# Gated linear attention and two mixtures: lo parts of the first weights on VectorE, gates cumulated in one float32 product, new ranks for the first phase

## The chip, the cores and the metric

The kernel runs on one core of a Trainium2 chip. The metric is the device time of one execution in microseconds (us), lower is better. The median of three runs before the change is 907.58 us (907.32 to 908.22).

## What is computed

Three steps follow each other: a gated linear attention, a first expert layer that every token passes, and a second one in which each of 3072 tokens goes to one of 8 experts.

```python
f = 1.0 / (1.0 + np.exp(-f_logit))            # q, k, v, f_logit: 4 x 8 x 768 x 48
for t in range(S):
    state = f[:, :, t, :, None] * state + einsum('bhd,bhe->bhde', k[:, :, t], v[:, :, t])
    y[:, :, t] = einsum('bhd,bhde->bhe', q[:, :, t], state)
x = y as 3072 x 384
x = ((x @ w_a) * (x @ w_b)) @ w_out           # 384 -> 1536 -> 384, given in float64
e = argmax(x @ w_gate); p = softmax's value at e
out = p * sigmoid(x @ w_output_gate)[e] * (relu(x @ w1[e]) @ w2[e])
```

## The kernel before, in words

Nearly every product is made of two parts. A float32 value is split into a hi part, which TensorE takes at full pace, and a lo part, the rest; three products (hi hi, hi lo, lo hi) stand for one. Making hi is a copy on ACT, making lo a subtraction.

**Attention** works on 24 tiles of 128 tokens (six chunks of four batches). Tile i loads f, q, k, v (`load_in`), takes the logarithm of its gates on ACT (`a_log`: Exp, then Ln at L720), cumulates them over the 128 tokens with a triangular matrix on TensorE (`a_cum`), makes the exponentials eq and ek on ACT, multiplies them with q and k on VectorE (`a_q`: qe, then ek), packs hi and lo into a tile z (`a_z`), which a DMA transposes (zT), adds to the state U (`a_kv`), makes scores in two halves (`a_score`: sm, Sh, Sl), multiplies them with v (`a_av`), and hands x as xh and xl to the first layer (`a_x`). The cumulation splits the logarithm into lh and ll (float16) and makes two products.

**First layer.** Two tiles are one token block j. For each of 12 blocks f of 128 columns, `m_ab` makes 18 products (L1011 to L1013) into a bank, ACT and VectorE make gf, ACT makes gh, GpSimd makes gl (L1027), and `m_out` makes six products (L1045 to L1047).

**Weights of the first layer** come as float64 words in 18 batches of 768 KB: a0, b0, then a1, b1, o0 and so on to o5. A batch is loaded by SP, two instructions on ACT (L587, L592) and two on VectorE (L594, L598) decode it to float32 in a tile `raw`, of which there are three, ACT makes hi, and GpSimd makes lo (L616 for a and b, L631 for o). `gates` then appends the columns of the router to wo: two transposes and products on TensorE for each o batch, and a small subtraction on VectorE (L658).

**Order.** Everything up to token block 1, tiles 0 to 5 and all 18 batches is the first phase. There `in_time` sets one order for each engine: it plays all threads against the costs written at each `yield op(...)`, and on each engine takes next the step with the smallest start plus `urge` times the thread's rank. Ranks come from the tables `T0` (tiles), `C0, CD` (batches), `X0, X1, DX` (products of blocks 0 and 1). Engines run their queues in order, so this order is what the chip does, whatever the costs are worth. From block 2 on, the products of a block are written out in order, with the attention of later tiles between them; a scheduler places what has no fixed order, and so pulls some loads and squares of `late_range` (a check on ranges of v, q, k) into the first phase.

Of the kernel before, what the change touches and what calls it, by code (L numbers as in the profile page):

```python
# [305 lines left out]
def kernel(  # L306
# [165 lines left out]
    def in_time(threads, urge):  # L472
# [9 lines left out]
        while live:  # L482
# [19 lines left out]
            if lands:  # L502
                end = max(end, wire - 3.0)
                wire = max(end, wire) + lands
            free[eng] = end
# [65 lines left out]
    def decoded(n):  # L571

        yield op("ACT", 1.1, ("raw", n), ("abs", n - 1), *free_ws(n - 3), gives=("abs", n))
        ws = held[n] = raw_tile()
        raw = doubles[n][:, : 4 * DM]
        if not wide:
            nc.scalar.activation(out=ws, in_=raw[:, : 2 * DM], func=AF.Copy, scale=2.0**WS)
            yield op("DVE", 0, ("abs", n), gives=("bits", n))
            return
        words = raw.bitcast(I32).rearrange("p (f c) -> p f c", c=2)  # L580
        top, low = words[:, :, 1], words[:, :, 0]
        byte = raw.bitcast(U8).rearrange("p (f c) -> p f c", c=8)[:, :, 3]
        bits = ws.bitcast(I32)

        nc.scalar.activation(  # L587
            out=ws, in_=top.bitcast(F32), func=AF.Abs, scale=2.0 ** (WS - 126), accum_out=st_w[:, n : n + 1]
        )

        yield op("ACT", 0.9, gives=("low", n))
        nc.scalar.activation(out=low, in_=byte, func=AF.Copy, scale=1.0 / 32, bias=-31.0 / 64)  # L592
        yield op("DVE", 1.05, ("low", n))
        nc.vector.scalar_tensor_tensor(  # L594
            out=bits, in0=bits, scalar=3, in1=low, op0=ALU.logical_shift_left, op1=ALU.bitwise_or
        )
        yield op("DVE", 1.1, gives=("bits", n))
        nc.vector.scalar_tensor_tensor(  # L598
            out=bits, in0=top, scalar=-(1 << 31), in1=bits, op0=ALU.bitwise_and, op1=ALU.bitwise_or
        )  # L600
# [6 lines left out]
    def conv_ab(n):  # L607
        nm, g = batches[n]
        yield from decoded(n)
        ws = held[n]  # L610
        yield op("ACT", 0.85, ("bits", n), ("hi", n - 1), gives=("hi", n))
        both = ring_tile("wab")
        hi, lo = both[:, : 2 * DM], both[:, 2 * DM :]
        nc.scalar.activation(out=hi, in_=ws, func=AF.Copy)
        yield op("POOL", 1.9, ("hi", n), gives=("lo", n))
        nc.gpsimd.tensor_tensor(out=lo, in0=ws, in1=hi.bitcast(F32), op=ALU.subtract)  # L616
        wab[nm, g] = [x.rearrange("p (k f) -> p k f", k=KD) for x in (hi, lo)]
# [3 lines left out]
    def conv_o(n):  # L621
# [7 lines left out]
        nc.scalar.activation(out=hi[:, :, :DM], in_=ws, func=AF.Copy)  # L629
        yield op("POOL", 1.9, ("hi", n), gives=("lo", n))  # L630
        nc.gpsimd.tensor_tensor(out=lo[:, :, :DM], in0=ws, in1=hi[:, :, :DM].bitcast(F32), op=ALU.subtract)  # L631

# [36 lines left out]
    def tl(name, shape, dt, bufs=1):  # L669
        return ab.tile(shape, dt, name=name, tag=name, bufs=bufs)  # L670
# [26 lines left out]
    xT = {}  # L697
    last_use = {"f": "ll", "v": "vv", "q": "qe", "k": "kx"}

# [14 lines left out]
    def a_log(i):  # L714
# [61 lines left out]
    def a_cum(i):  # L776
        yield op("PE", 0.45, ("ll", i), bank="ab" if i < NCB else "at", gives=("cum", i))
        s = st[i]
        pc = bank("ab" if i < NCB else "at")[:, : H * D].rearrange("p (h d) -> p h d", h=H)
        nc.tensor.matmul(pc, tri, s["lh"], start=True, stop=False)  # L780
        nc.tensor.matmul(pc, tri, s["ll"], start=False, stop=True)
        yield op("ACT", 0.57, ("cum", i), ("qe", i - 1), ("gd", i - 1), gives=("eq", i))
# [458 lines left out]

    T0 = [0, 10, 33, 61, 74, 87]
    C0, CD = 5.5, 3.9
    X0, X1, DX = 34.6, 82.4, 4.1
    threads = []
    for i in range(8):
        t0 = T0[i] if i < 6 else 100 + i
        for nm, t in (("f", 0), ("q", 1), ("k", 1), ("v", 2)):
            threads.append((t0 - 10 + t, load_in(i, nm)))
    for i in range(6):  # L1250
# [5 lines left out]
    for n in range(len(batches)):  # L1256
        t = C0 + CD * n
        threads.append((t - 6, raw_load(n)))
        threads.append((t, (conv_o if batches[n][0] == "o" else conv_ab)(n)))
        if batches[n][0] == "o":  # L1260
            threads.append((t - 10, gates(n)))

# [10 lines left out]
    threads.append((96, prefill()))  # L1273
    in_time(threads, 0.006)

# [307 lines left out]
    for j in range(2, NBLK):  # L1583
# [3 lines left out]
        for f in range(NF):  # L1587
# [134 lines left out]
```

## Time and profile before

| what | value |
|---|---|
| median of 3 runs | 907.58 us |
| profiled execution | 905.76 us |
| its span, first to last instruction | 904.1 us |
| TensorE busy | 828.6 us (92%) |
| VectorE busy | 533.4 us (59%) |
| ACT busy | 456.9 us (51%) |
| GpSimd busy | 349.9 us (39%) |

Shares are means over stages that differ: TensorE is nearly always busy behind the first 150 us, and idle in good part ahead of 50 us. The profile's names are PE for TensorE, PEld for its weight loads, DVE for VectorE, POOL for GpSimd, SP for the engine that issues most DMAs. A row's bracket gives the idle time in front of an instruction and what ended it.

### The profile page before, as it was taken

How to read it: one execution, taken by the hardware profiler on the slowest of the kernel's cores; microseconds unless marked ns; L12 is line 12 of the kernel's file. 1: busy time of each engine (PE TensorE's matmuls, PEld its weight loads, DVE VectorE, ACT ScalarE, POOL GpSimd, SP SyncE). 2: the span in 40 equal slices, each digit the busy share in tenths (PEclk: the TensorE clock that was granted, in tenths of full speed). 3: DMA queues.
4: the chain of work that ended last, by engine and by line, in shares of the span. 5: the costliest groups of instructions: out<-in, count | busy, mean ns of one | idle time of the engine just before them, and what ended most of it. 6: DMA issues, size and time to landing. Idle time of an engine off the chain costs nothing.

```text
span 904.1 us, 17986 instructions
## 1 busy us (share of the span) xinstructions
PE 828.6 (92%) x6733; PEld 781.0 (86%) x6733; DVE 533.4 (59%) x1217; ACT 456.9 (51%) x1068; POOL 349.9 (39%) x410
## 2 busy tenths in 40 slices
PE   2498788989999999999999999998979999999993
PEld 1388777989999999999999999998968999999993
DVE  8989853464646564747464656533537566666630
ACT  5777674444645454545454555333425434545520
POOL 4456542443536353544444444323252232221111
PEclk9999898999999999999999999999989999999997
DMA  9995394163626262534444442203166754575610
GB/s 227 299 244 142 74 203 91 31 89 48 119 45 121 39 126 39 106 60 94 72 86 80 77 88 53 43 27 120 57 149 204 198 157 121 182 191 158 172 60 23
DMA packets 261579, 102.06 MB, mean 113 GB/s; under 512 B 229032, under 2 KB 252933, under 8 KB 261482
## 3 DMA queue, kind: packets, MB, share of 16 engines
q1 hardware_dynamic: 256362, 90.76, 45.1%
q0 software_dynamic: 4320, 10.03, 3.9%
q8 instruction: 55, 0.90, 0.5%
q14 instruction: 42, 0.34, 0.1%
q10 hardware_dynamic: 800, 0.02, 0.1%
HBM read 67.10 MB, written 10.49 MB: 86 GB/s over the span
## 4 chain that ended last, share of the span: by engine, by line
PE 68%; DMA 10%; issue 8%; DVE 5%; POOL 3%; ACT 3%; SPq 1%; POOLq 0%; DVEq 0%; ACTq 0%
PE ps_ab L1011 11%; PE ps_ab L1012 10%; PE ps_ab L1013 10%; PE ps_out L1047 5%; PE ps_out L1045 5%; PE ps_out L1046 5%; PE ps_out L302 3%; DMA zT<-z 3%; PE ps_yk L302 3%; PE ps_at L902 3%; PE ps_ab L1402 3%; PE ps_ab L1403 2%; PE ps_ab L1404 2%; DMA raw<-in_moe_w_dram 2%; DMA turned<-halves 1%
## 5 line engine op out<-in xcount | busy, mean ns | idle before, releaser
L1011 PE MATMUL ps_ab<-xh,wab 128*128 128x256 f32 x864 | 252.5, 292 | 4.8 <-DVE gf L1019 3.4
L1012 PE MATMUL ps_ab<-xl,wab 128*128 128x256 f32 x864 | 248.0, 287 | 2.2 <-issue 1.1
L1013 PE MATMUL ps_ab<-xh,wab 128*128 128x256 f32 x864 | 247.2, 286 | 0.0
L1027 POOL TENSOR_TENSOR gl<-gf,gh 128x256 fp32r<-128x256 f32 x144 | 113.4, 790 | 221.3 <-ACT gh L1025 212.8
L1011 PEld LDWEIGHTS ps_ab<-xh,wab 128*128 128x128 f32 x864 | 166.4, 193 | 7.0 <-DVE gf L1019 3.5
L1012 PEld LDWEIGHTS ps_ab<-xl,wab 128*128 128x128 f32 x864 | 166.4, 193 | 3.9 <-issue 1.6
L1013 PEld LDWEIGHTS ps_ab<-xh,wab 128*128 128x128 f32 x864 | 166.5, 193 | 0.7 <-issue 0.5
L1019 DVE SCALAR_TENSOR_TENSOR gf<-ps_ab,asb 128x256 f32<-128x256 f32 x144 | 60.4, 420 | 83.1 <-ACT asb L1016 73.7
L1025 ACT ACTIVATE gh<-gf 128x256 fp32r<-128x256 f32 x144 | 59.9, 416 | 89.2 <-DVE gf L1019 85.7
L1047 PE MATMUL ps_out<-wo,gl 128*128 128x400 f32 x288 | 99.8, 354 | 3.8 <-POOL gl L1027 3.7
L1045 PE MATMUL ps_out<-wo,gh 128*128 128x400 f32 x288 | 101.9, 354 | 0.5 <-ACT gh L1025 0.5
L1046 PE MATMUL ps_out<-wo,gh 128*128 128x400 f32 x288 | 99.9, 347 | 0.9 <-DVE wo L658 0.9
L1016 ACT ACTIVATE asb<-ps_ab 128x256 f32<-128x256 f32 x144 | 54.8, 381 | 74.7 <-PE ps_ab L1013 73.8
L1476 POOL DMA_INDIRECT out_dram<-ys,tab x29 | 30.0, 1034 | 145.4 <-ACT ys L1471 139.0
L1402 PE MATMUL ps_ab<-xsh,wab 128*128 128x256 f32 (+5 forms) x216 | 73.5, 341 | 1.4 <-ACT xsh L1391 0.9
L1403 PE MATMUL ps_ab<-xsl,wab 128*128 128x256 f32 (+5 forms) x216 | 73.5, 340 | 0.1
L1404 PE MATMUL ps_ab<-xsh,wab 128*128 128x256 f32 (+5 forms) x216 | 73.2, 339 | 0.0
L1186 DVE TENSOR_TENSOR wab<-raw,wab 128x768 fp32r<-128x768 f32 x48 | 46.5, 970 | 41.2 <-ACT wab L302 33.6
L1416 ACT ACTIVATE h<-ps_ab 128x256 fp32r<-128x256 f32 (+5 forms) x72 | 34.8, 483 | 69.9 <-PE ps_ab L1404 53.6
L1420 DVE SCALAR_TENSOR_TENSOR h<-ps_ab,h 128x64 fp32r<-128x64 f32 (+5 forms) x96 | 41.2, 450 | 35.5 <-ACT h L1416 33.2
L917 DVE TENSOR_TENSOR Sl<-sm,Sh 128x512 f16<-128x512 f32 x48 | 37.0, 771 | 38.3 <-ACT Sh L915 38.3
L1047 PEld LDWEIGHTS ps_out<-wo,gl 128*128 128x128 f32 x288 | 54.0, 189 | 5.9 <-POOL gl L1027 5.3
(246 smaller groups left out, 1829.4 us busy)
## 6 DMA issues: line engine op xcount, KB each, us to landing
raw<-in_moe_w_dram SPq DMA_DIRECT2D x64, 384.0 KB
in_f<-in_f_logit_dram SPq DMA_DIRECT2D x24, 192.0 KB
in_q<-in_q_dram SPq DMA_DIRECT2D x24, 192.0 KB
in_k<-in_k_dram SPq DMA_DIRECT2D x24, 192.0 KB
in_v<-in_v_dram SPq DMA_DIRECT2D x24, 192.0 KB
wab<-in_moe_w_a_dram SPq DMA_DIRECT2D x6, 768.0 KB
wab<-in_moe_w_b_dram SPq DMA_DIRECT2D x6, 768.0 KB
wo<-in_moe_w_out_dram SPq DMA_DIRECT2D x6, 768.0 KB
```

The source lines that it names most:

```text
L1011: nc.tensor.matmul(pab[:, a], wh[:, kk, o : o + P], xh[:, kk], start=(kk == 0), stop=False)
L1012: nc.tensor.matmul(pab[:, a], wh[:, kk, o : o + P], xl[:, kk], start=False, stop=False)
L1013: nc.tensor.matmul(pab[:, a], wl[:, kk, o : o + P], xh[:, kk], start=False, stop=(kk == KD - 1))
L1019: nc.vector.scalar_tensor_tensor(out=gf, in0=pab[:, 1], scalar=2.0**-WS, in1=asb, op0=ALU.mult, op1=ALU.mult)
L1025: nc.scalar.activation(out=gh, in_=gf, func=AF.Copy)
L1027: nc.gpsimd.tensor_tensor(out=gl, in0=gf, in1=gh.bitcast(F32), op=ALU.subtract)
L1045: nc.tensor.matmul(o, gh[:, ts], wh[:, u], start=(f == 0), stop=False)
L1046: nc.tensor.matmul(o, gh[:, ts], wl[:, u], start=False, stop=False)
L1047: nc.tensor.matmul(o, gl[:, ts], wh[:, u], start=False, stop=(f == NF - 1))
L1402: nc.tensor.matmul(ph, wh[:, kk, o : o + P], sh[:, kk, us], start=(kk == 0), stop=False)
L1403: nc.tensor.matmul(ph, wh[:, kk, o : o + P], sl[:, kk, us], start=False, stop=False)
L1404: nc.tensor.matmul(ph, wl[:, kk, o : o + P], sh[:, kk, us], start=False, stop=(kk == KD - 1))
```

## The change

Four things change.

The 18 lo subtractions of the first layer's weights (L616, L631) go from GpSimd to VectorE, same operands, same result.

For tiles 0 to 5 the cumulation multiplies the float32 logarithm with a float32 copy of the triangular matrix in one product; lh and ll are made for later tiles only. The copy, `tri_f`, is one more small instruction on GpSimd at the start.

The tables of ranks and some costs for `in_time` are set anew: `T0`, `C0, CD`, `X1, DX`, the loads' lead, `urge`; a transposing DMA is reckoned to end 2.9 us behind the loads in flight.

`late_range` is called two blocks later.

```diff
             if lands:
-                end = max(end, wire - 3.0)
-                wire = max(end, wire) + lands
+                end = max(end, wire + 2.9 if us > 3 else wire - 3.0)
+                wire = end if us > 3 else max(end, wire) + lands
...
-        yield op("POOL", 1.9, ("hi", n), gives=("lo", n))
-        nc.gpsimd.tensor_tensor(out=lo, in0=ws, in1=hi.bitcast(F32), op=ALU.subtract)
+        yield op("DVE", 1.0, ("hi", n), gives=("lo", n))
+        nc.vector.tensor_tensor(out=lo, in0=ws, in1=hi.bitcast(F32), op=ALU.subtract)
...
-        yield op("POOL", 1.9, ("hi", n), gives=("lo", n))
-        nc.gpsimd.tensor_tensor(out=lo[:, :, :DM], in0=ws, in1=hi[:, :, :DM].bitcast(F32), op=ALU.subtract)
+        yield op("DVE", 1.0, ("hi", n), gives=("lo", n))
+        nc.vector.tensor_tensor(out=lo[:, :, :DM], in0=ws, in1=hi[:, :, :DM].bitcast(F32), op=ALU.subtract)
...
+    tri_f = tl("tri_f", [P, P], F32)
+    nc.gpsimd.tensor_copy(out=tri_f, in_=tri)
...
         nc.scalar.activation(out=f, in_=f, func=AF.Ln, scale=c_st, bias=c_st)
+        if i < NPE:
+            return
         yield op("DVE", 0.4, ("ln", i), ("cum", i - 1), gives=("lh", i))
...
+        early = i < NPE
+        yield op("PE", 0.7, ("ln" if early else "ll", i), bank="ab" if i < NCB else "at", gives=("cum", i))
...
+        if early:
+            nc.tensor.matmul(pc, tri_f, s["f"], start=True, stop=True)
+        else:
+            nc.tensor.matmul(pc, tri, s["lh"], start=True, stop=False)
+            nc.tensor.matmul(pc, tri, s["ll"], start=False, stop=True)
...
-    T0 = [0, 10, 33, 61, 74, 87]
-    C0, CD = 5.5, 3.9
-    X0, X1, DX = 34.6, 82.4, 4.1
+    T0 = [0, 6, 31, 61, 76, 82]
+    C0, CD = 6.2, 3.85
+    X0, X1, DX = 34.6, 96, 3.86
...
-            if f == 6:
-                late_range(j - 2)
+            if f == 6 and j > 3:
+                late_range(j - 4)
```

In the order that comes of it, three places bear on what follows. Lines of the changed kernel are up to eight higher.

VectorE, from qe of tile 1 (L800 before, L808 now) on; z_177 is the tile that its transpose reads. Before:

```order
L800 TENSOR_TENSOR qe<-in_q,eq 128x384
L802 TENSOR_TENSOR ek<-in_k,ek 128x384
L917 TENSOR_TENSOR Sl<-sm,Sh 128x4x128
L813 CAST z_177<-ek 128x4x2x48
L909 TENSOR_TENSOR sm<-ps_at,mask 128x512
L815 TENSOR_TENSOR z_177<-ek,z_177 128x4x2x48
L594 SCALAR_TENSOR_TENSOR raw<-raw,wab 128x768
L917 TENSOR_TENSOR Sl<-sm,Sh 128x4x128
L598 SCALAR_TENSOR_TENSOR raw<-wab,raw 128x768
L879 SCALAR_TENSOR_TENSOR U_184<-ps_ab,g_182 128x192
L819 CAST z_177<-qe 128x4x2x48 x2
L821 TENSOR_TENSOR z_177<-qe,z_177 128x4x2x48
```

The same place now:

```order
L808 TENSOR_TENSOR qe<-in_q,eq 128x384
L810 TENSOR_TENSOR ek<-in_k,ek 128x384
L756 CAST vv<-in_v 128x384
L821 CAST z_177<-ek 128x4x2x48
L917 TENSOR_TENSOR sm<-ps_at,mask 128x512
L887 SCALAR_TENSOR_TENSOR U_184<-ps_ab,g_182 128x192
L823 TENSOR_TENSOR z_177<-ek,z_177 128x4x2x48
L925 TENSOR_TENSOR Sl<-sm,Sh 128x4x128
L827 CAST z_177<-qe 128x4x2x48
L917 TENSOR_TENSOR sm<-ps_at,mask 128x512
L827 CAST z_177<-qe 128x4x2x48
L829 TENSOR_TENSOR z_177<-qe,z_177 128x4x2x48
```

The decode of a1 no longer stands between qe and the last part of z; the two lo subtractions of a0 and b0 stand just ahead of the first row. On TensorE the cumulation of tile 1 now stands ahead of both halves of the scores of tile 0; before it stood between them.

SP, behind the transpose of tile 0 (z_176). Before, a1, b1, o0, then:

```order
L840 DMA g_182<-gd 48x4x1 x2
L792 DMA gd<-eq 1x384
L567 DMA wab<-in_moe_w_a_dram 128x3x256
L567 DMA wab<-in_moe_w_b_dram 128x3x256
L302 DMA in_f<-in_f_logit_dram 128x8x48
L840 DMA g_183<-gd 48x4x1 x2
L302 DMA in_q<-in_q_dram 128x8x48
L824 DMA_TRANSPOSE zT<-z_177 128x20x128
```

Now:

```order
L800 DMA gd<-eq 1x384
L567 DMA wab<-in_moe_w_b_dram 128x3x256
L567 DMA wo<-in_moe_w_out_dram 128x2x384
L302 DMA in_f<-in_f_logit_dram 128x8x48
L848 DMA g_183<-gd 48x4x1
L832 DMA_TRANSPOSE zT<-z_177 128x20x128
L848 DMA g_183<-gd 48x4x1
L567 DMA wab<-in_moe_w_a_dram 128x3x256
```

The loads of a2 and b2 (the wab rows of the first piece) stood ahead of the transpose of tile 1; the last row of the second piece is that of a2, now behind it. The wab and wo rows of the second piece are b1 and o0.

VectorE where the last two batches, o4 and o5, are decoded. Before:

```order
L594 SCALAR_TENSOR_TENSOR raw<-raw,wo 128x768
L598 SCALAR_TENSOR_TENSOR raw<-wo,raw 128x768
L909 TENSOR_TENSOR sm<-ps_at,mask 128x512
L1019 SCALAR_TENSOR_TENSOR gf<-ps_ab,asb 128x256
L594 SCALAR_TENSOR_TENSOR raw<-raw,wo 128x768
L917 TENSOR_TENSOR Sl<-sm,Sh 128x4x128
L598 SCALAR_TENSOR_TENSOR raw<-wo,raw 128x768
```

Now:

```order
L594 SCALAR_TENSOR_TENSOR raw<-raw,wo 128x768
L598 SCALAR_TENSOR_TENSOR raw<-wo,raw 128x768
L594 SCALAR_TENSOR_TENSOR raw<-raw,wo 128x768
L631 TENSOR_TENSOR wo<-raw,wo 128x2x384
L887 SCALAR_TENSOR_TENSOR U_187<-ps_at,g_183 128x192
L598 SCALAR_TENSOR_TENSOR raw<-wo,raw 128x768
L1027 SCALAR_TENSOR_TENSOR gf<-ps_ab,asb 128x256
L917 TENSOR_TENSOR sm<-ps_at,mask 128x512
L1027 SCALAR_TENSOR_TENSOR gf<-ps_ab,asb 128x256
L631 TENSOR_TENSOR wo<-raw,wo 128x2x384
```

Both batches now stand ahead of the scores of tile 3 (sm), with their subtractions among them; before, the scores stood between the two.

## Rows read from the trace of the kernel before

**Rows 1.** Stretches: length, busy of PE, PEld, DVE, ACT, POOL, PEclk, DMA share, GB/s.
```profile
0.00:49.80 49.80, 17.93 (x159) 12.24 (x159) 43.69 (x89) 34.26 (x60) 22.32 (x31) 1.00 1.05 270
49.80:123.30 73.50, 64.68 (x516) 60.32 (x516) 58.20 (x79) 53.91 (x126) 43.23 (x33) 0.93 0.65 148
...
150.00:640.00 490.00, 483.75 (x4501) 458.58 (x4498) 271.72 (x699) 247.50 (x646) 212.12 (x276) 1.00 0.40 75
```

**Rows 2.** Timeline of TensorE: start, us, engine, line, operation, tiles, idle before it.
```profile
18.77 1.15 PE L902 MATMUL ps_at<-zT 128*128 128x128 f16 x8 [5.68 <-DMA zT<-z]
...
49.82 0.58 PE L1012 MATMUL ps_ab<-xl,wab 128*128 128x256 f32 x1 [0.86 <-DVE xl L984]
...
123.74 0.38 PE L1012 MATMUL ps_ab<-xl,wab 128*128 128x256 f32 x1 [0.19 <-DVE xl L984]
...
139.70 0.61 PE L902 MATMUL ps_at<-zT 128*128 128x128 f16 x4 [3.31 <-DMA zT<-z]
```

**Rows 3.** The chain of waits in the first phase: start, us, what.
```profile
18.25 8.38 DMA wo<-in_moe_w_out_dram
...
28.68 7.45 DMA zT<-z
...
108.47 1.82 POOL wo L631
```

**Rows 4.** Timeline of VectorE: decodes and a cast.
```profile
13.09 0.96 DVE L598 SCALAR_TENSOR_TENSOR raw<-wab,raw 128x768 int32<-128x768 int32 x1
...
15.17 2.45 DVE L598 SCALAR_TENSOR_TENSOR raw<-wab,raw 128x768 int32<-128x768 int32 x1
...
105.98 1.48 DVE L598 SCALAR_TENSOR_TENSOR raw<-wo,raw 128x768 int32<-128x768 int32 x1
...
108.58 1.93 DVE L752 CAST vv<-in_v 128x384 f16<-128x384 f32 x1
```

**Rows 5.** Timeline of GpSimd at the first subtraction.
```profile
15.00 1.81 POOL L616 TENSOR_TENSOR wab<-raw,wab 128x768 fp32r<-128x768 f32 x1 [4.69 <-ACT wab L614]
```

**Rows 6.** GpSimd by line, 0 to 124 us: count, busy, mean ns, idle before.
```profile
L616 POOL TENSOR_TENSOR wab<-raw,wab 128x768 fp32r<-128x768 f32 x12 | 24.9, 2074 | 30.4 <-ACT wab L614 27.1 <-ACT wo L656 3.3
L631 POOL TENSOR_TENSOR wo<-raw,wo 128x768 fp32r<-128x768 f32 x6 | 13.4, 2233 | 8.6 <-ACT wo L629 6.8 <-PE ps_at L902 1.8
L1027 POOL TENSOR_TENSOR gl<-gf,gh 128x256 fp32r<-128x256 f32 x12 | 13.3, 1110 | 9.5 <-ACT gh L1025 5.4 <-PE ps_yk L654 4.1
```

**Rows 7.** Costliest groups of the page: the same subtraction in the second layer.
```profile
L1186 DVE TENSOR_TENSOR wab<-raw,wab 128x768 fp32r<-128x768 f32 x48 | 46.5, 970 | 41.2 <-ACT wab L302 33.6
```

**Rows 8.** Timeline of VectorE around tile 1.
```profile
17.55 0.35 DVE L723 CAST lh<-in_f 128x384 f16<-128x384 f32 x1
18.00 0.56 DVE L726 TENSOR_TENSOR ll<-in_f,lh 128x384 f16<-128x384 f32 x1
...
21.32 0.68 DVE L800 TENSOR_TENSOR qe<-in_q,eq 128x384 f32<-128x384 f32 x1
...
28.05 0.56 DVE L821 TENSOR_TENSOR z<-qe,z 128x384 f16<-128x384 f32 x1
...
34.22 2.56 DVE L594 SCALAR_TENSOR_TENSOR raw<-raw,wab 128x768 int32<-128x768 int32 x1
```

**Rows 9.** Timeline of TensorE: a cumulating product and three float32 transposes.
```profile
80.33 0.34 PE L780 MATMUL ps_at<-lh,tri 128*128 128x384 f16 x1
...
85.28 0.49 PE L642 MATMUL ps_yk<-idn,raw 128*128 128x128 f32 x3
```

**Rows 10.** Timeline of ACT: Ln and eq of tile 1.
```profile
15.37 0.71 ACT L720 ACTIVATE in_f<-in_f,c_st 128x384 f32<-128x384 f32 x1
...
20.71 0.58 ACT L784 ACTIVATE eq<-ps_ab,c_b 128x384 f32<-128x384 f32 x1 [1.80 <-PE ps_ab L781]
```

**Rows 11.** SP's queue: the transpose of tile 1.
```profile
28.68 5.43 SPq L824 DMA_TRANSPOSE zT<-z  x1
```

**Rows 12.** Waits from 80 to 150 us: in total, times, longest.
```profile
DVE wo L658 <- ACT wo L656: 7.8, 3, 5.1
```

More of the change, by code (lines that the diff above doesn't have):

```diff
@@ L571, in decoded @@
     def decoded(n):
-        yield op("ACT", 1.1, ("raw", n), ("abs", n - 1), *free_ws(n - 3), gives=("abs", n))
+        yield op("ACT", 1.08, ("raw", n), ("abs", n - 1), *free_ws(n - 3), gives=("abs", n))
         ws = held[n] = raw_tile()
@@ L592, in decoded @@
         nc.scalar.activation(out=low, in_=byte, func=AF.Copy, scale=1.0 / 32, bias=-31.0 / 64)
-        yield op("DVE", 1.05, ("low", n))
+        yield op("DVE", 1.0, ("low", n))
         nc.vector.scalar_tensor_tensor(
@@ L596, in decoded @@
         )
-        yield op("DVE", 1.1, gives=("bits", n))
+        yield op("DVE", 1.05, gives=("bits", n))
         nc.vector.scalar_tensor_tensor(
@@ L697 @@
     xT = {}
-    last_use = {"f": "ll", "v": "vv", "q": "qe", "k": "kx"}
+    last_use = {"f": "cum", "v": "vv", "q": "qe", "k": "kx"}
     def load_in(i, names):
@@ L776, in a_cum @@
     def a_cum(i):
-        yield op("PE", 0.45, ("ll", i), bank="ab" if i < NCB else "at", gives=("cum", i))
+        early = i < NPE
+        yield op("PE", 0.7, ("ln" if early else "ll", i), bank="ab" if i < NCB else "at", gives=("cum", i))
         s = st[i]
         pc = bank("ab" if i < NCB else "at")[:, : H * D].rearrange("p (h d) -> p h d", h=H)
-        nc.tensor.matmul(pc, tri, s["lh"], start=True, stop=False)
-        nc.tensor.matmul(pc, tri, s["ll"], start=False, stop=True)
+        if early:
[3 more added lines that the diff above has]
+            nc.tensor.matmul(pc, tri, s["ll"], start=False, stop=True)
         yield op("ACT", 0.57, ("cum", i), ("qe", i - 1), ("gd", i - 1), gives=("eq", i))
@@ L1248 @@
         for nm, t in (("f", 0), ("q", 1), ("k", 1), ("v", 2)):
-            threads.append((t0 - 10 + t, load_in(i, nm)))
+            threads.append((t0 - 11.8 + t, load_in(i, nm)))
     for i in range(6):
@@ L1260 @@
         if batches[n][0] == "o":
-            threads.append((t - 10, gates(n)))
+            threads.append((t - 9.4, gates(n)))
     def product(j, f):
@@ L1273 @@
     threads.append((96, prefill()))
-    in_time(threads, 0.006)
+    in_time(threads, 0.0021)
     cnt_a = const("cnt_a", [P, 1], F32)
```

## The prediction, made before the change had run

> **What bounds the kernel now.** I read the busy time by stretch first, then the chain of waits, then the timelines of the engines that the chain names. By stretch [rows 1], TensorE is busy for 483.75 of the 490.00 us from 150 to 640: there the end is set by TensorE's work, and the change does not touch that work. From 49.8 to 123.3 it is busy for 64.68 of 73.50 us at a mean granted clock of 0.93, while VectorE is busy for 58.20. So what the change is worth is how much earlier TensorE gets through the first phase. I take one mark for it: the first product of token block 1, which stands right behind the last output product of block 0. Before, its second matmul, which waits for xl of tile 3, starts at 123.74 [rows 2]. The first product of block 0 runs freely from 49.82, when xl of tile 1 comes [rows 2]. Behind both marks the order on TensorE is almost that of before, so the end moves with the second mark.
>
> The chain of waits in the first phase goes through the transpose of tile 1 (28.68, 7.45 us), then for long through VectorE, and near the second mark through GpSimd's subtraction of wo, 1.82 us from 108.47 [rows 3]. VectorE's busy time there is not all work. The decode at 13.09 takes 0.96 us, the same instruction at 15.17 takes 2.45 [rows 4], and GpSimd's subtraction runs from 15.00 to 16.81 [rows 5]: 16.81 plus 0.81 is the end of the VectorE instruction. VectorE stood still until GpSimd was through. I went along VectorE's timeline and took for each instruction the excess over the shortest of its form: 16 run beside an L616 or L631 and lose 21.3 us together, the first is that of 15.17 (1.51), the last the cast of 108.58, 1.93 instead of 0.35 [rows 4]. Seven of them, 7.3 us, lie ahead of 49.8, and nine, 14.0 us, between the marks. Nine more run beside a gl subtraction only and lose 3.9 us, the last is that of 105.98 with 0.54.
>
> The Trainium skill states this in "SBUF — State Buffer", Who interferes with whom: a VectorE instruction with two inputs in SBUF contends with a GpSimd instruction that reads SBUF, one of them waits for the whole of the other, and the order of issue decides which. This trace agrees (2.45 beside 0.96). What the rule says against the change is the third rival.
>
> **Part 1: 18 subtractions from GpSimd to VectorE.** It takes away 12 of 2074 ns and 6 of 2233 ns on GpSimd [rows 6], 38.3 us, most of it waited for by nobody. On VectorE it adds 18 of 0.95 us, 17.1 us: the same operation and shape in the second MoE takes 970 ns in the mean of 48 [rows 7], stretched ones among them, and a decode of the same width 0.96 [rows 4]. It gives back the 21.3 us of standing still. So VectorE's own account gains 4 us, and a lo part is there 1 us sooner.
>
> **Part 2: the cumulated gates as one float32 product.** For six tiles lh (0.35) goes from VectorE, and ll too for tiles 0 to 3 (0.56) [rows 8]; for tiles 4 and 5 ll goes from GpSimd. Together 2.1 and 2.2, 4.3 us less on VectorE. TensorE has one float32 product in place of two in float16 of 0.34 [rows 9], which overlap, about 0.5 us for the pair. A float32 product of 384 columns does not occur. The lower bound is the three float32 transposes of 128 columns, 0.49 together [rows 9]; for the upper bound I take four times one of the float16 products, 1.4. I take 0.6, near the row in float32: 0.1 more in each of six. Since VectorE is late anyway at five of them I count 0.5 us in all; the bounds are 0 and 5.
>
> **Part 3: ranks.** Two places decide.
>
> Tile 1. Before, VectorE starts on qe of tile 1 at 21.32 and ends its last z part at 28.61 [rows 8], and the transpose goes out at 28.68. Between them stand two decodes, U and three score instructions. qe waits for eq, which ACT begins at 20.71 behind the cumulation, and the cumulation stands on TensorE behind scores of tile 0, which wait for their transpose until 18.77 [rows 2]; its input, the Ln at 15.37, ended at 16.08 [rows 10]. In the change the cumulation stands ahead of those scores, and no decode between qe and z. Ln at 16.1, product and eq by 17.5, two lo subtractions on VectorE until 18 and qe at 18.3; from there twelve instructions of 0.35 to 0.68 [rows 8] make 6 us: z at 24.3 instead of 28.6. With the same 7.45 us the transpose lands at 31.8 instead of 36.1. Then eight score products (four took 0.61 [rows 2], so 1.2 us), and on VectorE the 16 instructions that the order has from the first sm to xl of tile 1: five of 0.95, four of 0.68, the rest of 0.17 to 0.56, 10.6 us. That is 43.6. One cost goes against it: on SP the load of a2 stood ahead of the transpose and now stands behind it, at some 30 with the 5.43 us for which SP was held there [rows 11]. Its decode on VectorE began at 34.22 before [rows 8] and would now be wanted at 36 to 37. The load takes between 2.9 us (0.79 MB at the 270 GB/s of this stretch [rows 1]) and the 8.38 that o0 took in the crowd [rows 3]; I take 5, since the crowd ahead is then mostly through, and with two instructions of 0.9 on ACT the decode is just about in time. I take 44 for the first mark, against 49.8; the bounds are 41 (all in time) and 47 (a2 late, or the transpose slower in the crowd of loads).
>
> Between the marks. VectorE loses the 14.0 us of standing still. It gains 13 of the 18 subtractions (five now lie ahead of xl of tile 1), 12.4; less two lh and one ll (1.3); and six instructions of tile 4 (0.35 to 0.56, together 2.7) now stand ahead of the second mark. Sum: -0.2. VectorE's idle time there is 15.3 us (73.50 less 58.20), and 7.8 of it is three waits of the wo remainder for ACT near the end [rows 12], in the stretch where GpSimd's in-order queue works through L631, ll and gl. With the decode over sooner and gl no longer queued behind a subtraction, I let 7 of the 15.3 us return, most of the three waits; the bounds are 0 and 12. So this stretch goes from 73.5 to 66.3. TensorE cannot do it in less than about 60: 64.68 busy, less what the 0.93 cost.
>
> Behind the second mark I count nothing. The 3.31 us for which TensorE waits on the transpose of tile 4 [rows 2] may go or come again, since its z is done only just ahead of the mark. The checks on the ranges, now tied to later blocks, stand on SP and ACT behind the transpose of tile 3 as before: nothing. Bounds for both, 4 us gained to 3 lost.
>
> **Sum.** 5.8 for the earlier start, 7.2 between the marks, less 0.5 for float32: 12.5 us. The profiled execution took 905.76 us (span 904.1 and 1.66 around it), 1.8 below the median of the runs, 907.58. 905.76 - 12.5 = 893.3, and 1.8 for the median: 895.
>
> **Rivals.**
> First, all of it comes: the start at 42, TensorE's 60 us between the marks and no wait for tile 4's transpose, 7.8 + 13.5 + 3 = 24 us, or 883. For it: in the stretch VectorE is the engine that the chain names most. Against: the chain hands work on through ACT and DMA too, which the change leaves as they are. A middle of it, some 18 us and 889, is more likely than the end.
> Second, only the start comes: weights are what the stretch waits for. The transpose of tile 1 ahead of a2 and b2 puts off 13 of the 18 weight batches, and what is won is waited away. Then the gain is the 5.8 us or less: 902. For it: SP's queue goes in order. Against: the last decode starts only at 105.98 [rows 4], and the DMA engines are busy for no more than 0.65 of the stretch [rows 1].
> Third, GpSimd and VectorE still block each other. Of GpSimd's 13.3 us of gl ahead of the mark [rows 6], 3.9 now cost VectorE time; the 18 added subtractions have two SBUF inputs, and meet them more often. At the worst another 9.4 us: 904; at half of it 900. The page named above says this of issue order.
> Fourth, slower: the standing still was not paid by the chain. The price is 17.1 us of new VectorE work less the 4.3 us of lh and ll, 12.8 us, and it decides as soon as less than that of the 21.3 us lay on the chain and the ranks give nothing: with none of it 920, with 9 us of it 911. Against: the decodes that stood still are named by the chain itself.
>
> **Chances.** 0.55 for 889 to 899 around 895, 0.15 for the first rival below that, 0.13 for the second and 0.10 for the third (both 899 to 905), 0.07 for the fourth. What this measurement can tell from no change is 0.2%, 1.8 us, so 905.8 to 909.4 is the same: 0.04, which comes from the ends of the second to fourth; faster 0.90, slower 0.06. The range that holds eight in ten is 886 to 904.
>
> **What would show it.** Right: no VectorE decode of more than 1.5 us; xl of tile 1 at 42 to 46; the last L631 by 100; the first product of block 1 at 107 to 114; from there the same distances to the end. Wrong: L616 on VectorE well over 1 us, or gl at much over 1.1 us; TensorE waiting for the transpose of tile 1 until after 35; VectorE idle ahead of decodes of a2 to a4, which would say that the loads bind; the second mark at 118 or later.

## The result, and the profile after

| | median of runs | ratio to the kernel before |
|---|---|---|
| before | 907.45 us (906.29 to 908.22) | |
| change | 898.42 us (894.51 to 2011.81, 4 runs) | 0.9882, 95% [0.9838, 0.9926] |
| change, run again | 898.13 us (893.02 to 904.04, 10 runs) | 0.9900, 95% [0.9863, 0.9937] |

The change is faster: both intervals lie below 1, and the ratios are worth 10.7 and 9.1 us, where 12.5 were forecast. One of the first four runs took 2011.81 us, with TensorE's products at half their pace throughout; it is in the median 898.42 (the three others have a median of 895.47) but not in the ratio. The profile read here is of the kernel run again: 897.54 us with a span of 895.8, against 905.76 and 904.1 before. The ten runs of that row differ by up to 11.0 us, so a sum of a few us taken from two profiled executions tells of these two. Behind the cumulation the line numbers of the changed kernel are eight higher than before (L1019 to L1021 are the products of `m_ab`).

The stretches that answer to [rows 1], in the same columns:

```profile
0.00:49.80 49.80, 23.36 (x180) 17.13 (x181) 41.33 (x93) 32.92 (x59) 8.85 (x26) 1.00 1.04 262
49.80:123.30 73.50, 69.10 (x657) 63.18 (x655) 65.93 (x123) 63.35 (x154) 26.73 (x28) 0.98 0.81 181
150.00:640.00 490.00, 477.69 (x4400) 453.12 (x4399) 270.79 (x716) 241.97 (x636) 206.62 (x266) 0.99 0.42 75
```

TensorE does 5.4 us more work in the first stretch and 4.4 more in the second. In the third, where the prediction saw only work, it is busy for 477.69 us instead of 483.75: 6 us more of idle time, at a clock a little lower. That is the first sign that something won earlier is given back.

TensorE's timeline at the places of [rows 2] (start, us, engine, line, operation, tiles, idle before it):

```profile
32.15 1.15 PE L910 MATMUL ps_at<-zT 128*128 128x128 f16 x8 [3.87 <-DMA zT<-z]
...
46.01 0.41 PE L1020 MATMUL ps_ab<-xl,wab 128*128 128x256 f32 x1
...
112.28 0.57 PE L1019 MATMUL ps_ab<-xh,wab 128*128 128x256 f32 x1
112.70 0.28 PE L1020 MATMUL ps_ab<-xl,wab 128*128 128x256 f32 x1
...
131.21 0.72 PE L910 MATMUL ps_at<-zT 128*128 128x128 f16 x8 [1.44 <-DMA zT<-z]
```

The first mark (the first product with xl) went from 49.82 to 46.01, the second from 123.74 to 112.70: 3.8 and 11.0 us earlier. The wait for tile 4's transpose went from 3.31 to 1.44. VectorE's part in it, in groups by line (count, busy us, mean ns, idle before); the first two rows are of the kernel before, the others of the change:

```profile
L598 DVE SCALAR_TENSOR_TENSOR raw<-wab,raw 128x768 int32<-128x768 int32 x12 | 19.4, 1617 | 0.2
L598 DVE SCALAR_TENSOR_TENSOR raw<-wo,raw 128x768 int32<-128x768 int32 x6 | 7.1, 1180 | 0.1
```

```profile
L598 DVE SCALAR_TENSOR_TENSOR raw<-wab,raw 128x768 int32<-128x768 int32 x12 | 13.0, 1086 | 0.2
L616 DVE TENSOR_TENSOR wab<-raw,wab 128x768 fp32r<-128x768 f32 x12 | 12.2, 1013 | 1.1 <-ACT wab L614 1.0
L598 DVE SCALAR_TENSOR_TENSOR raw<-wo,raw 128x768 int32<-128x768 int32 x6 | 6.7, 1110 | 0.1
L631 DVE TENSOR_TENSOR wo<-raw,wo 128x768 fp32r<-128x768 f32 x6 | 5.7, 949 | 0.6 <-ACT wo L629 0.6
```

The subtractions cost VectorE 12.2 + 5.7 = 17.9 us (17.1 forecast). One form of decode alone gives 6.4 us back; its mean falls from 1617 to 1086 ns, and none of them takes longer than 1.49 us.

**Where it was lost again.** TensorE at the cumulation of tile 6, at the end of product 28 (the last `m_ab` matmul of it; a product is one `m_ab`, twelve to a block), and at the scores of tile 6. First the kernel before, then the change:

```profile
170.13 0.34 PE L780 MATMUL ps_at<-lh,tri 128*128 128x384 f16 x1
...
189.51 0.28 PE L1013 MATMUL ps_ab<-xh,wab 128*128 128x256 f32 x1
...
194.83 0.72 PE L902 MATMUL ps_at<-zT 128*128 128x128 f16 x8
```

```profile
161.51 0.34 PE L788 MATMUL ps_at<-lh,tri 128*128 128x384 f16 x1
...
171.41 0.28 PE L1021 MATMUL ps_ab<-xh,wab 128*128 128x256 f32 x1
...
183.56 1.15 PE L910 MATMUL ps_at<-zT 128*128 128x128 f16 x8 [6.78 <-DMA zT<-z]
```

At product 28 the change is 18.1 us ahead (189.51 less 171.41), more than at the mark. (These us ahead are called the lead from here on.) Then it waits 6.78 us. The distance from the cumulation to the scores had been 24.7 us before and is now 22.1, 6.78 of them waiting: TensorE has only 15.3 us of other work between them, since the cumulation now stands behind product 25, where the program's text has it, and before it had been drawn ahead of product 23. What has to fit into that distance is the way from the cumulation to the landed transpose. The chain of waits, and SP's queue (queue, line, operation), in the change:

```profile
167.87 15.60 DMA zT<-z
```

```profile
163.50 0.35 SPq L1067 DMA_DIRECT2D x2d<-xr  x1
...
164.95 0.38 SPq L302 DMA_DIRECT2D in_v<-in_v_dram  x1
165.38 0.69 SPq L302 DMA_DIRECT2D in_f<-in_f_logit_dram  x1
...
167.87 4.16 SPq L832 DMA_TRANSPOSE zT<-z  x1
```

and in the kernel before:

```profile
176.17 3.08 SPq L824 DMA_TRANSPOSE zT<-z  x1
182.98 0.89 SPq L1059 DMA_DIRECT2D x2d<-xr  x2
183.93 0.45 SPq L302 DMA_DIRECT2D in_v<-in_v_dram  x1
```

From the cumulation to the issue are 6.0 to 6.4 us in both. But the transpose takes 15.60 us, twice the 7.81 of tile 1's in the crowd of the first phase: it is issued behind the rows of x2d and the loads of tile 8, ahead of which it stood before.

### The profile page after: what moved, and what is told of

The parts are those of the page before. It is cut to its first block, busy times and chain, and to the rows that moved or that the text cites. A ratio compares the mean times of both kernels' runs of the same rounds, so it can differ in the third digit from the quotient of the medians.

```text
span 2010.1 us, 17953 instructions
## 1 busy us (share of the span) xinstructions
PE 1969.6 (98%) x6733; PEld 1666.8 (83%) x6733; DVE 512.0 (25%) x1225; ACT 460.5 (23%) x1068; POOL 305.6 (15%) x391
## 5 line engine op out<-in xcount | busy, mean ns | idle before, releaser
L1019 PE MATMUL ps_ab<-xh,wab 128*128 128x256 f32 x864 | 463.2, 536 | 0.0
L1021 PE MATMUL ps_ab<-xh,wab 128*128 128x256 f32 x864 | 459.9, 532 | 0.0
L1020 PE MATMUL ps_ab<-xl,wab 128*128 128x256 f32 x864 | 459.3, 532 | 0.0
L1021 PEld LDWEIGHTS ps_ab<-xh,wab 128*128 128x128 f32 x864 | 374.1, 433 | 1.5 <-issue 1.5
L1020 PEld LDWEIGHTS ps_ab<-xl,wab 128*128 128x128 f32 x864 | 362.9, 420 | 13.6 <-issue 12.6
L1019 PEld LDWEIGHTS ps_ab<-xh,wab 128*128 128x128 f32 x864 | 358.5, 415 | 12.7 <-issue 9.4
L1054 PE MATMUL ps_out<-wo,gh 128*128 128x400 f32 x288 | 202.0, 701 | 0.0
L1053 PE MATMUL ps_out<-wo,gh 128*128 128x400 f32 x288 | 201.8, 701 | 0.0
L1055 PE MATMUL ps_out<-wo,gl 128*128 128x400 f32 x288 | 198.7, 699 | 0.0
L1410 PE MATMUL ps_ab<-xsh,wab 128*128 128x256 f32 (+5 forms) x216 | 146.0, 677 | 0.0
L1411 PE MATMUL ps_ab<-xsl,wab 128*128 128x256 f32 (+5 forms) x216 | 145.0, 671 | 0.0
L1412 PE MATMUL ps_ab<-xsh,wab 128*128 128x256 f32 (+5 forms) x216 | 144.7, 670 | 0.0
L1053 PEld LDWEIGHTS ps_out<-wo,gh 128*128 128x128 f32 x288 | 110.8, 385 | 22.9 <-issue 19.6
L1054 PEld LDWEIGHTS ps_out<-wo,gh 128*128 128x128 f32 x288 | 114.7, 398 | 16.7 <-issue 13.7
L1412 PEld LDWEIGHTS ps_ab<-xsh,wab 128*128 128x128 f32 x216 | 80.0, 370 | 23.0 <-issue 21.4
```

The lines of the kernel that those rows point to most:

```text
L1019: nc.tensor.matmul(pab[:, a], wh[:, kk, o : o + P], xh[:, kk], start=(kk == 0), stop=False)
L1020: nc.tensor.matmul(pab[:, a], wh[:, kk, o : o + P], xl[:, kk], start=False, stop=False)
L1021: nc.tensor.matmul(pab[:, a], wl[:, kk, o : o + P], xh[:, kk], start=False, stop=(kk == KD - 1))
L1053: nc.tensor.matmul(o, gh[:, ts], wh[:, u], start=(f == 0), stop=False)
L1054: nc.tensor.matmul(o, gh[:, ts], wl[:, u], start=False, stop=False)
L1055: nc.tensor.matmul(o, gl[:, ts], wh[:, u], start=False, stop=(f == NF - 1))
```

## The experiments

Each ratio is to the kernel before, on the same chip. The experiments ran on three chips, so versions are compared by their ratios.

**One part alone.** The change itself again, then the kernel before with nothing but the engine of the subtractions changed, then the change with these back on GpSimd, then the change with the ranks of before.

> The changed kernel once more, for a profile to read. Theory (VectorE was held by GpSimd, and the new ranks bring tile 1 sooner): about 895 us; xl of tile 1 at 42 to 46, the first product of block 1 at 107 to 114. Rival (the loads bind): the mark at 115 or later and VectorE idle ahead of decodes.

> The kernel before, in its own order, with the 18 lo subtractions on VectorE. Theory (standing still was paid): VectorE gets 17.1 us more work and 21.3 us back, and gl does not queue behind the subtractions: 4 to 8 us less than before, 899 to 903. Rival (the standing still was not paid): 5 to 13 us more, 912 to 920.

```diff
-        nc.gpsimd.tensor_tensor(out=lo, in0=ws, in1=hi.bitcast(F32), op=ALU.subtract)
+        nc.vector.tensor_tensor(out=lo, in0=ws, in1=hi.bitcast(F32), op=ALU.subtract)
...
-        nc.gpsimd.tensor_tensor(out=lo[:, :, :DM], in0=ws, in1=hi[:, :, :DM].bitcast(F32), op=ALU.subtract)
+        nc.vector.tensor_tensor(out=lo[:, :, :DM], in0=ws, in1=hi[:, :, :DM].bitcast(F32), op=ALU.subtract)
```

> The changed kernel, same ranks and same order on VectorE, TensorE and SP in the first phase, with the 18 lo subtractions on GpSimd again. Theory: VectorE loses some 20 us standing still and saves 17.1, and lo and gl come later: 900 to 906. If the engine of the subtractions does not matter: 895. Rival (the subtractions are a burden on VectorE): under 890.

```diff
-        nc.vector.tensor_tensor(out=lo, in0=ws, in1=hi.bitcast(F32), op=ALU.subtract)
+        nc.gpsimd.tensor_tensor(out=lo, in0=ws, in1=hi.bitcast(F32), op=ALU.subtract)
...
-        nc.vector.tensor_tensor(out=lo[:, :, :DM], in0=ws, in1=hi[:, :, :DM].bitcast(F32), op=ALU.subtract)
+        nc.gpsimd.tensor_tensor(out=lo[:, :, :DM], in0=ws, in1=hi[:, :, :DM].bitcast(F32), op=ALU.subtract)
```

> The changed kernel with all the ranks of before (T0, C0, CD, X0, X1, DX, leads, urge, the transpose's reckoning). Theory: the earlier start is lost, 5 to 7 us: 900 to 902, and xl of tile 1 at 48 to 50. If the ranks give nothing: 895. If they give nearly all: 905 to 908.

```diff
-                end = max(end, wire + 2.9 if us > 3 else wire - 3.0)
-                wire = end if us > 3 else max(end, wire) + lands
+                end = max(end, wire - 3.0)
+                wire = max(end, wire) + lands
...
-    T0 = [0, 6, 31, 61, 76, 82]
-    C0, CD = 6.2, 3.85
-    X0, X1, DX = 34.6, 96, 3.86
+    T0 = [0, 10, 33, 61, 74, 87]
+    C0, CD = 5.5, 3.9
+    X0, X1, DX = 34.6, 82.4, 4.1
...
-            threads.append((t0 - 11.8 + t, load_in(i, nm)))
+            threads.append((t0 - 10 + t, load_in(i, nm)))
...
-            threads.append((t - 9.4, gates(n)))
+            threads.append((t - 10, gates(n)))
...
-    in_time(threads, 0.0021)
+    in_time(threads, 0.006)
```

| kernel | median | ratio, 95% |
|---|---|---|
| change | 898.13 us | 0.9900 [0.9863, 0.9937] |
| subtractions on VectorE, old order | 902.08 us | 0.9926 [0.9897, 0.9956] |
| new order, subtractions on GpSimd | 902.85 us | 0.9937 [0.9906, 0.9968] |
| change with old ranks | 902.21 us | 0.9944 [0.9904, 0.9985] |

Each part alone gives about half, 5 to 6 us of 907.75: moving the subtractions pays by itself, and the fourth rival (slower) is refuted. The two parts (the second holds the float32 product and the later `late_range` too) add up to 10.6 us where the change gives 9.6; within the intervals that is their sum. At the second mark the shares are not even: the subtractions alone bring it from 123.74 to 116.30, the new order alone to 121.60, both to 112.70.

Two mechanisms show in the traces behind what the subtractions are worth, and their shares are not told apart. One is VectorE standing still: with the subtractions on GpSimd again, the twelve decodes of the first form (L598, for a and b) take 17.0 us instead of 13.0. The other is GpSimd's queue, in which gl stands behind the subtractions. In that kernel TensorE waits for gl in the first phase, here from 45 to 123 us (in total, times, longest), where in the change it waits 0.2 us:

```profile
PE ps_out L1055 <- POOL gl L1035: 4.8, 3, 2.3
```

In the kernels with the new order TensorE waits at tile 6, with the subtractions on GpSimd too:

```profile
192.50 1.15 PE L910 MATMUL ps_at<-zT 128*128 128x128 f16 x8 [6.74 <-DMA zT<-z]
```

The kernel with the old order and the subtractions on VectorE has only smaller ones behind product 28, the longest 2.36 us. With the old ranks in the changed kernel, xl of tile 1 comes at 56.78, later than the 48 to 50 expected and later than in the kernel before (49.21), yet the second mark at 120.14: the old ranks do not bring the old order back, so this run does not price the ranks of tile 1 alone. The intervals of the three variants overlap that of the change, so of each part's share only the direction is settled.

**The old cumulation.**

> The change, but the cumulated gates of the first six tiles are made as before, from two float16 parts (lh, ll) in two float16 products. That puts 4.3 us of lh and ll back on VectorE and takes one float32 product of the first six tiles off TensorE. Theory (VectorE and the way from Ln to qe count in the first phase): first product of block 1 2 to 5 us later than in the change, 900 to 902. Rival (VectorE has slack of its own there): the mark within 1 us of 112.3 and the time 897 to 899.

```diff
-    last_use = {"f": "cum", "v": "vv", "q": "qe", "k": "kx"}
+    last_use = {"f": "ll", "v": "vv", "q": "qe", "k": "kx"}
...
-        if i < NPE:
-            return
...
-        early = i < NPE
-        yield op("PE", 0.7, ("ln" if early else "ll", i), bank="ab" if i < NCB else "at", gives=("cum", i))
+        early = False
+        yield op("PE", 0.45, ("ln" if early else "ll", i), bank="ab" if i < NCB else "at", gives=("cum", i))
```

899.83 us, ratio 0.9928 [0.9899, 0.9958]: some 2.5 us more than the change by the ratios, which the intervals do not separate from nothing. In the trace the theory holds at the mark: the first mark is the same (45.86 and 46.01), the first product of block 1 starts at 117.32 instead of 112.28, 5.0 us later. But `in_time` also makes another order of the other steps (the fourth cumulation starts at 84.01 instead of 57.91), so how much of the 5.0 us belongs to the 4.3 us less on VectorE is open. TensorE's float32 product stands in the change's trace as two overlapping records each (line, count, busy, mean ns; four of the six tiles):

```profile
L786 PE MATMUL ps_at<-in_f,tri_f 128*128 128x384 f32 x8 | 4.4, 635 | 0.0
```

The three later pairs take 0.91 us each (the first of them from 57.91 to 58.82), the three in the first 50 us 1.65 each, where 0.6 was taken and 0.49 to 1.4 were the bounds. One of the long ones stands on the chain ahead of the first mark; more of that below.

**What makes the transpose of tile 6 late.** First the loads out of its way:

> The change, but in the one loop in question the loads of tiles 8 and 9 (x2d, v, f, q, k) are issued on SyncE behind the transposes of tiles 6 and 7 instead of ahead of them. In the change the transpose of tile 6 took 15.60 us from issue to landing, behind those loads, and TensorE waited 6.78 us for it. Theory (the loads ahead of it in the queue make it late): it lands about 5.5 us after its issue as before, TensorE does not wait for it, the end comes 6 to 9 us earlier, 889 to 892. Rival (the transpose is late because its z is late, or the DMA engines are slow there whatever is ahead): it takes over 12 us again, and the time stays at 897 to 899. Second rival: the loads, now later, make the z of tile 8 late and the same wait stands there: 896 to 899, with the wait moved by two token tiles.

```diff
                 if at[t][n] == f and steps[n]:
+                    if n == 2 and i0 == 6:
+                        continue
                     run(steps[n](i0 + t) or ())
+            if i0 == 6 and f == at[t][5] + 1:
+                run(steps[2](i0 + t) or ())
```

893.58 us, ratio 0.9855 [0.9827, 0.9882]. Its timeline of TensorE:

```profile
179.51 0.80 PE L910 MATMUL ps_at<-zT 128*128 128x128 f16 x8 [2.48 <-DMA zT<-z]
...
187.19 0.71 PE L910 MATMUL ps_at<-zT 128*128 128x128 f16 x8 [2.05 <-DVE U L302]
```

Both the theory and the second rival had a part: the transpose comes 4 us earlier, though with nothing ahead of it but x2d it still takes over 11 us, and a second wait stands 8 us later, behind a load of gates that took 12.19 us. So the queue's order cannot be the only cause.

Then the range checks' loads, which the change issues early, kept at their place:

> The change, but the loads and squares of the range checks are kept at the place in the program where their step runs, instead of being issued earlier by the scheduler. In the change ScalarE stands in the first phase waiting for such loads (3.89 and 4.14 us on the chain at 93.37 and 108.61). If these waits decide when the first product of token block 1 starts, it starts at 108 to 110 instead of 112.3, and the end comes 1 to 3 us earlier: 895 to 897. Rival (something else is as late, and the lead is given back later anyway): 898 with the mark at 112.

```diff
-            nc.sync.dma_start(x, src[b, :, c * P : (c + 1) * P, :].rearrange("h p d -> p h d"))
-            squares(i, n, x, 1.0, x)
+            in_order(tc, nc.sync.dma_start)(x, src[b, :, c * P : (c + 1) * P, :].rearrange("h p d -> p h d"))
+            in_order(tc, nc.scalar.activation)(
+                out=x, in_=x, func=AF.Square, scale=1.0, accum_out=st_qkv[:, i, n : n + 1]
+            )
```

> Both edits: loads of tiles 8 and 9 behind the transposes of tiles 6 and 7, and the loads and squares of the range checks kept in place. If the two act in different places their gains add: 6 to 9 and 1 to 3 us, 887 to 890. Rival (the first wait only becomes the next one, as the lead grows): no better than the better of the two alone.

922.94 us (ratio 1.0186 [1.0162, 1.0209]), and with both edits 921.76 (1.0174 [1.0152, 1.0196]): a clear miss. The first product of block 1 does start earlier, as expected, at 109.90 instead of 112.28 (with both edits at 110.5): so in the change the early loads of the checks, for which the prediction counted nothing, cost the mark 2.4 us. But the three loads of a check now stand ahead of a transpose in each block of the main loop. The chain and TensorE's timeline at one of them:

```profile
335.73 9.59 DMA zT<-z
```

```profile
345.37 1.14 PE L912 MATMUL ps_at<-zT 128*128 128x128 f16 x8 [4.29 <-DMA zT<-z]
```

Five such waits of 3.06 to 4.32 us, 18.0 together, follow from 291 to 502, where the change has none over 0.54. A load that is nobody's hurry was cheap while the DMA engines were crowded anyway, and dear ahead of a transpose.

**The cumulation's place.** Tile 6's front half handed to the planner of the first phase, which puts its cumulation behind product 18:

> The change, with the front half of token tile 6 (gates, cumulation, qe, kx, z, transpose, vs, u) handed to the planner of the first phase, so that its cumulation stands on TensorE behind product 18 instead of behind product 25, and its transpose on SyncE ahead of the x2d stores and the loads of tiles 8 and 9. Theory: in the change the cumulation stands 5 products, 15.3 us of TensorE, ahead of the scores of tile 6, and the way from the cumulation to the landed transpose takes 6 + 15.6 us, so TensorE waits 6.78 us; in the kernel before it stood 7 products ahead (170.13 to 194.83) and nothing waited. With 11 products between them nothing waits, the lead of 18.1 us at product 28 is kept to 12 or more, and the time is 886 to 891. Rival: the lead is lost to what comes next in any case (the transpose or the loads of tiles 7 and 8), a wait of 4 us or more stands at the scores of tile 7 or 8, and the time is 893 to 898.

```diff
+                    if i0 + t == 6 and n in (0, 1, 3, 4, 5, 6):
+                        continue
...
+    T6 = 116
...
+    for t, gen in (
+        (0, a_log(6)), (3, a_v(6)), (2, a_cum(6)), (3, a_q(6)), (4, a_z(6)), (6, a_vs(6)), (4, a_u(6)), (4, a_uh(6)),
+    ):
+        threads.append((T6 + t, gen))
```

and the kernel before, with that one cumulation kept where the change has it:

> The kernel before, with one thing changed: the cumulation of token tile 6 is kept on TensorE at its place in the program, behind product 25, where it stands in the change, instead of behind product 22; its transpose then stands on SyncE behind the x2d stores and the loads of tile 8, as in the change. Theory (this order, not the subtractions or the gates, costs the wait): TensorE waits 5 to 8 us for the transpose of tile 6, and the time is 910 to 915. Rival (the wait in the change comes from having 18 us of lead, VectorE and GpSimd being as late as before): no wait over 2 us, 906 to 909.

```diff
-        nc.tensor.matmul(pc, tri, s["lh"], start=True, stop=False)
-        nc.tensor.matmul(pc, tri, s["ll"], start=False, stop=True)
+        (in_order(tc, nc.tensor.matmul) if i == 6 else nc.tensor.matmul)(pc, tri, s["lh"], start=True, stop=False)
+        (in_order(tc, nc.tensor.matmul) if i == 6 else nc.tensor.matmul)(pc, tri, s["ll"], start=False, stop=True)
```

The kernel before with the late cumulation takes 914.63 us, ratio 1.0030 [1.0003, 1.0057]. Its chain, and TensorE:

```profile
188.32 14.98 DMA zT<-z
```

```profile
203.35 1.15 PE L902 MATMUL ps_at<-zT 128*128 128x128 f16 x8 [6.86 <-DMA zT<-z]
```

So the wait of 6.8 us needs neither the lead nor the subtractions on VectorE: this order brings it, in the same size, into the kernel before. The time grows by less than the wait, 2.7 us by the ratio [0.3, 5.2]. The early cumulation, 898.21 us, ratio 0.9860 [0.9822, 0.9898], removes that wait, but the rival was right: the next thing in the stretch is late. TensorE's timeline and ScalarE's, and the chain:

```profile
188.00 1.12 PE L910 MATMUL ps_at<-zT 128*128 128x128 f16 x8 [6.85 <-DVE U L302]
```

```profile
185.62 0.52 ACT L720 ACTIVATE in_f<-in_f 128x384 f32<-128x384 f32 x1 [4.44 <-DMA in_f<-in_f_logit_dram]
```

```profile
170.60 15.00 DMA in_f<-in_f_logit_dram
```

A load of gates, 192 KB, takes 15.00 us; ScalarE's queue stands behind the Exp that wants it, and with it the evictions, VectorE and TensorE. Whatever is in flight from 170 to 185 is late.

**Why the DMA engines are slow there.** The DMA view of the change from 160 to 200, a slice each us (busy share in tenths, then GB/s), and GpSimd's timeline:

```profile
DMA  0000568999929899599999699710000139496000
GB/s 0 0 0 10 197 191 164 228 202 200 194 41 289 154 82 45 39 16 12 19 5 11 51 160 192 131 28 2 0 0 0 2 71 76 100 290 135 0 0 0
```

```profile
168.83 1.21 POOL L1161 DMA_INDIRECT slots<-info,di  x1 [1.18 <-DVE sm L1153]
170.35 0.98 POOL L1161 DMA_INDIRECT slots<-info,di  x1 [0.31 <-issue]
```

From 174 on the engines are busy and move 5 to 82 GB/s for eight us, where they moved some 200 from 164 to 171. That begins some 5 us behind the first scatter to the slot table (a scatter is `DMA_INDIRECT`, which writes 128 rows of 8 bytes to places that the data give). So the routing of blocks 0 and 1 was put five products later, where no tile's loads are under way:

> The change, with the routing of token blocks 0 and 1 (ranks and the first two pairs of scatters to the slot table) put five products later, behind products 31 and 33, where no load of a token tile is under way. In every trace so far the DMA engines are busy but move under 60 GB/s for some 8 to 12 us, beginning about 5 us behind the first scatter (168.83 in the change), and what is in flight then lands after 12 to 16 us. Theory (the first scatters among the loads make them slow): loads and the transpose of tile 6 run at 150 GB/s or more there, the transpose lands within 8 us of 167.9, TensorE waits under 1 us, the time is 888 to 892. Rival (the slow stretch comes from the loads and the x2d stores themselves): the transpose takes 15 us again, the wait of 6.8 us stays, the time is 896 to 899.

```diff
-                if f in (1, 3):
-                    r_rank(f // 2)
-                    r_send(f // 2)
+                if f in (6, 8):
+                    r_rank(f // 2 - 3)
+                    r_send(f // 2 - 3)
```

> Both: the front half of token tile 6 planned in the first phase (its cumulation behind product 18) and the first two pairs of scatters put five products later. Theory: nothing waits between products 25 and 33, the lead of 14 to 18 us at product 28 is kept, and the time is 884 to 889, the fastest of all. Rival (the slow stretch of the DMA engines comes from the loads): the load of gates for tile 8 takes 15 us again, VectorE and TensorE wait for it behind ScalarE's queue as they did with tile 6 alone, 893 to 898.

892.56 us, ratio 0.9819 [0.9783, 0.9854], and together with the early cumulation 891.25, ratio 0.9804 [0.9769, 0.9839]. The DMA view, GpSimd and TensorE of the first:

```profile
DMA  0001679999995799470100299900000810000010
GB/s 0 0 2 45 187 210 216 212 206 196 248 245 89 150 196 214 89 154 1 1 0 0 46 214 217 191 3 1 1 1 0 165 31 0 0 0 0 0 16 0
```

```profile
186.85 1.22 POOL L1161 DMA_INDIRECT slots<-info,di  x1 [0.32 <-DVE di L1150]
```

```profile
175.99 0.72 PE L910 MATMUL ps_at<-zT 128*128 128x128 f16 x8
```

The same loads in the same order (the transpose is issued at 167.33, behind them) now run at 89 to 248 GB/s until they are through at 178. The transpose has landed by 175.99, 8.7 us after its issue, and TensorE does not wait for it; its next wait, for the transpose of tile 7, is 1.40 us at 187.92. This bears the theory out: loads, transpose and cumulation stand in the order of the change, only the scatters and the small steps that compute their ranks stand elsewhere, and the wait of 6.78 us is gone. The theory's sizes are met nearly (888 to 892 us, landing within 8). Both versions beat the ten runs of the change above, since their intervals lie below 0.9863; against the first runs, 0.9882 [0.9838, 0.9926], the intervals overlap a little. Between the two, and against 893.58 for the loads alone, nothing is told apart; the 884 to 889 hoped for of both together was missed.

## Why the prediction was right, and where it was wrong

**First mark: right in its steps but for the float32 product, 2 us short.** z of tile 1 was to be done at 24.3; the chain has the transpose issued at 24.30, and the scores start at 32.15 (31.8 forecast):

```profile
24.30 7.81 DMA zT<-z
```

From there 11.8 us were reckoned to the first mark, and it took 13.9. VectorE's instructions there are hardly longer than forecast, but it waits in between for ScalarE (1.15 and 0.79 us) and TensorE (0.61), which the sum left out. The longest of these goes back to the float32 product of part 2: it stands between the two halves of tile 1's scores and takes 1.65 us instead of 0.6, ScalarE waits for it with eq, and Sh, for which VectorE waits, stands behind eq in ScalarE's queue. TensorE's and ScalarE's timelines:

```profile
33.23 1.65 PE L786 MATMUL ps_at<-in_f,tri_f 128*128 128x384 f32 x2
```

```profile
34.91 0.58 ACT L792 ACTIVATE eq<-ps_at,c_b 128x384 f32<-128x384 f32 x1 [2.10 <-PE ps_at L786]
```

The gain was 3.8 us instead of 5.8.

**Between the marks: right.** 73.9 us (49.82 to 123.74) became 66.7 (46.01 to 112.70): 7.2 us, the forecast of 7.2. The three waits of the wo remainder, 7.8 us in [rows 12], are one of 1.1:

```profile
DVE wo L658 <- ACT wo L656: 1.1, 1, 1.1
```

The last L631 starts at 99.93 (by 100 forecast). In the fixed window from 49.8 to 123.3 VectorE is busy for 65.93 us instead of 58.20 [rows 1]: its idle time fell from 15.3 to 7.6 us, where 7 were let return (the window reaches 10.6 us beyond the change's second mark).

**The rule on two inputs in SBUF.** The third rival priced it at 5 to 9 us. The 54 decodes and subtractions together take 55.7 us (the four groups above, and two of L594 with 11.4 and 6.7), some 5 more than 54 times the shortest of 0.94; the decodes alone had lost more than that before (19.4 instead of 11.3 in one form). The Trainium skill's "SBUF — State Buffer", Who interferes with whom, names the contention, and [rows 4, 5] showed it at its largest; with the long subtractions gone from GpSimd, little of it is left: no decode takes longer than 1.49 us, where 2.56 was the longest.

**"Behind the second mark I count nothing": wrong, twice.** The step rested on "the order on TensorE is almost that of before". It is not at one place: the cumulation of tile 6 stands behind product 25 instead of ahead of product 23. The stretch from the second mark to the end of product 28, first before, then in the change, with the two that follow there:

```profile
123.30:189.80 66.50, 60.69 (x539) 56.65 (x539) 35.37 (x91) 35.83 (x105) 25.92 (x37) 0.95 0.49 98
```

```profile
112.30:171.70 59.40, 56.93 (x514) 54.48 (x513) 28.23 (x82) 33.75 (x101) 20.63 (x29) 1.00 0.58 105
...
171.70:183.50 11.80, 5.08 (x61) 4.55 (x60) 7.55 (x15) 2.72 (x8) 7.33 (x9) 0.80 1.18 70
183.50:200.00 16.50, 16.44 (x158) 15.23 (x159) 6.69 (x13) 7.22 (x16) 3.61 (x6) 0.83 0.45 68
```

The change needs 59.4 us (112.3 to 171.7) for what took 66.5, at a clock of 1.00 instead of 0.95 and with 2.5 us idle instead of 5.8: 7.1 us more gained, where the bound was 4. Then 9.8 us are lost, where the bound was 3: 11.0 + 7.1 - 9.8 = 8.3, the difference of the two spans. The wait is 6.78 of the 9.8. In the stretch with it the granted clock is 0.80 in the mean and in the next 0.83, so parts of both ran at the lower of the two levels, after an idle TensorE; product 30, right behind the wait, takes 4.2 us, where one before it took 2.3, 1.9 more. The kernel before is not at full pace there either: its product 30 has two pauses for which the profile shows no reason:

```profile
198.37 0.28 PE L1011 MATMUL ps_ab<-xh,wab 128*128 128x256 f32 x1 [0.83 <-issue]
...
199.80 0.28 PE L1012 MATMUL ps_ab<-xl,wab 128*128 128x256 f32 x1 [1.15 <-issue]
```

So 6.7 us of the lead go here: it is 11.4 at the end of product 30 (200.20 less 188.84). The last 3.1 go piece by piece, with gains between: the lead is 12.6 at the end of product 36, 10.7 behind a pause of the same kind (1.70 us at 242.38), 9.4 at the last scores, 10.2 at TensorE's last instruction (889.83 less 879.65) and 8.3 at the end.

Of the 4.2 us that are missing between the two profiled executions (12.5 less 8.3) the first mark is 2.0 and this step 2.7, less the 0.5 counted apart for float32. That the forecast came so near is luck in this step, since its two errors, 7.1 and 9.8, nearly cancel; of the first rival ("all of it comes", 883 to 889) most had come by product 28.

## What to carry to other kernels

When a stage gets faster, follow the lead beyond the stage: list the places where the order of instructions behind it differs, and for each compare the work that stands between a producer and its consumer with the producer's whole way, DMA included. Here one instruction's place, with the scatters among the loads, was enough for a wait of 6.8 us, and the kernel before, with that instruction moved, had it as well. Moving the one late thing makes the next one late as long as the cause (slow DMA engines) stays; ask what all late things in a stretch have in common.

## What the runs showed of the hardware that was not expected

Two scatters of 128 rows of 8 bytes (168.83 and 170.35) among loads of 192 KB made the DMA engines move 5 to 82 GB/s for eight us instead of about 200; without them the same loads ran at 89 to 248. The kernel before has the same dip at another time (24 to 88 GB/s in slices of one us from 189 to 197, its first scatter at 185.62), and every other experiment with the first scatters among the loads has one too. In later blocks the loads were through 2 to 3 us behind the first scatter, ahead of the 5 us at which the dip began, and no dip of that length shows there; whether only the first scatters do this, and by which mechanism, was not tried.
